# Retention and a squared-ReLU feed-forward on one core: outputs of the paired units in two steps, one weight block cast in four slices, and the decay of q moved to the evacuation of x

## The chip, the cores and the metric

The kernel runs on one core of a Trainium2 chip. A core has TensorE (PE; its weight loads are listed apart as PEld), VectorE (DVE), ScalarE (ACT), GpSimd (POOL) and SyncE (SP), which issues the transfers here. All of them run their own instruction streams in order and meet at semaphores. The metric is the device time of one execution in microseconds (us). Six executions of the kernel before took 293.09 to 294.34 us, with a median of 293.74.

## The reference, cut to what matters

```python
# q, k, v: (8, 8, 576, 64) float32;  w_in: (512, 2048);  w_out: (2048, 512)
scores = matmul(q, k^T) / sqrt(64)
gamma  = 1 - 2 ** (-5 - arange(8))                       # one decay per head
Dmat   = where(i >= j, gamma ** (i - j), 0)              # causal, decaying
attn   = matmul(scores * Dmat, v)                        # (8, 8, 576, 64)
x      = attn.transpose(0, 2, 1, 3).reshape(4608, 512)
h      = x @ w_in                                        # (4608, 2048)
out    = (max(h, 0) ** 2) @ w_out                        # (4608, 512)
```

## The kernel before, in words

**Units and groups.** The 4608 rows are cut into 36 units of 128 rows: four full chunks of a batch, and, for each two batches, a tail unit with the last 64 rows of both. Two units make a group, so there are 18 groups. Units 0 to 7 (groups 0 to 3, `PAIRED = 8`) are "paired": two chunks of one batch are loaded together with even and odd rows side by side, cast, transposed on TensorE and treated as one. From unit 8 on, GpSimd casts k and q, multiplies v by a decay, and k and q are transposed by a transfer.

**Retention.** The decay gamma^(i-j) is split into gamma^i on the side of q and gamma^(-j) on the side of v (`vdec`, applied as v is cast). Within a chunk the scores (`psc`) are masked by VectorE to `rT` (or `rx`) and multiplied by v; across chunks a state R, updated by VectorE from the sums of k and v (`psS`), is multiplied by q. Both parts are added up in PSUM as `psO`, in 64x64 quads. Then `psO` is evacuated to `xT` in fp16. For paired groups the factor gamma^i (`gam_f`) is applied there, by VectorE (line 543). For later groups q itself is multiplied by it (`qdec`, lines 363 to 369, two GpSimd instructions per unit), and the evacuation is a plain cast, one unit of the group by ScalarE and the other by VectorE (lines 707 to 713).

**Outputs of a paired group.** One TensorE task (`fo`, line 521) does the inter part that reads the state after the pair's first unit or before it for the crossed row halves (`inter(1)`), a drain, the intra part (32 quads), and the other inter part (`inter(0)`). It waits for all masks and for R.

**Feed-forward.** `ph` (line 831) multiplies `w_in` by `xT`, sixteen blocks of four matmuls per group, 128x256 each. ScalarE takes the ReLU to `rl`; ScalarE or VectorE squares it to `gT`. For groups 0 and 1 the second product `po` is a plain one (line 869), one unit's sixteen matmuls after the other's. From group 2 on it is a Strassen scheme (line 920) with seven products, for which VectorE forms four sums (`gS`, line 897) and, once, four sums of weights (`wT`, line 782).

**Loads and weights.** SyncE issues the loads in one written order, `FIRST`: k, q and v of units 0 and 2 with the weight blocks w0 to w7 among and behind them, then units 4 and 6. w0 to w3 are the blocks of `w_in`, w4 to w7 those of `w_out`, 1 MB each. They and the paired loads share a ring of four staging buffers (`wst`), so a load is issued when the casts of the load four places ahead have ended. Each weight block is cast in two halves, one by GpSimd and one by ScalarE (lines 318 to 325).

**Order of work.** The order on every engine comes from a planner, `Schedule`: tasks carry an engine, a key, a planned duration, dependencies and resources, and a simulated list scheduler takes, whenever an engine is free, the ready task of the lowest key. The order found is then written out, and the hardware runs each engine's list in order. Forty warm-up matmuls (line 248) have the highest key and are taken when TensorE has nothing else. A changed duration or key can thus change the order of all that follows.

Of the kernel before, what the change touches and what calls it, by code (L numbers as in the profile page):

```python
# [9 lines left out]
FP32 = mybir.dt.float32  # L10
# [93 lines left out]
def kernel(  # L104
# [13 lines left out]
    P = 128  # L118
# [56 lines left out]
    lnscale = const.tile([P, 1], FP32, name="lnscale")  # L175
    nc.vector.memset(lnscale, math.log(scale))

    vdec, qdec = {}, {}

    def make_vdec(kind, pos):  # L180
        t = const.tile([P, H], FP32, name=f"vdl_{kind}")
        nc.vector.tensor_scalar(out=t, in0=lnrow, scalar1=pos, scalar2=None, op0=ALU.mult)
        if kind in ("full", "tail"):
            e = qdec[kind] = const.tile([P, H], FP32, name=f"qdec_{kind}")
            nc.scalar.activation(out=e, in_=t, func=ACTF.Exp, scale=-1.0)
        d = const.tile([P, H], FP32, name=f"vdec_{kind}")
        nc.scalar.activation(out=d, in_=t, func=ACTF.Exp, bias=lnscale, scale=1.0)
        vdec[kind] = d
# [30 lines left out]
    gam_f = const.tile([P, NP, P], FP32, name="gam_full")  # L219
    for hp in range(NP):  # L220
        nc.scalar.activation(out=gam_f[:, hp, :], in_=iota_f, func=ACTF.Exp, scale=lncol[:, hp:hp + 1])
    dec128 = const.tile([P, NP], FP32, name="dec128")
    nc.scalar.activation(out=dec128, in_=lnrow_R, func=ACTF.Exp, scale=128.0)

# [66 lines left out]
    def add_load_pair(name, u):  # L291
# [3 lines left out]
        def fn():  # L295
            if name != "q":
# [3 lines left out]
        loaded[name, u] = loaded[name, u + 1] = dma_task(0, 1.81 if loaded else 2.9, fn, acq=("wst",) if name != "q" else (),  # L300
                                                         after=2.1 + LAG.get(name + str(u), 0.0))

    def add_weight(i):
        fb = i % 4

        def fn():
            if i < 4:
                t = stage.tile([P, NP, 512], FP32, name=f"wi{fb}", tag="wst")
                nc.sync.dma_start(out=t, in_=w_in[:, fb * 512:(fb + 1) * 512].rearrange("(m p) f -> p m f", p=P))
            else:  # L310
                t = stage.tile([P, 4, DM], FP32, name=f"wo{fb}", tag="wst")
                nc.sync.dma_start(out=t, in_=w_out[fb * 512:(fb + 1) * 512, :].rearrange("(n p) m -> p n m", p=P))
            tile_of["w", i] = t
        t = dma_task(0, 2.75, fn, acq=("wst",), after=2.1 + LAG.get(f"w{i}", 0.0))
        dst = w_in16[:, :, fb * 512:(fb + 1) * 512] if i < 4 else w_out16[:, fb * 4:(fb + 1) * 4, :]

        halves = []
        for j, eng in enumerate(("POOL", "ACT")):
            rows, sl = (slice(0, 4), slice(256 * j, 256 * j + 256)) if i == 0 else (slice(2 * j, 2 * j + 2), slice(0, 512))

            def fc(eng=eng, rows=rows, sl=sl):
                s = tile_of["w", i]
                (nc.gpsimd.tensor_copy if eng == "POOL" else nc.scalar.copy)(out=dst[:, rows, sl], in_=s[:, rows, sl])  # L323
            key = -50 + i if i or j == 0 else -17.5
            halves.append(add(eng, key, 1.05 if eng == "POOL" else 1.0, fc, deps=[t]))
        sched.free("wst", halves)
        wcast[i] = halves

# [18 lines left out]
    def half(x):  # L347
        return slice(64 * x, 64 * x + 64)

    def add_unit(u, base):  # L350

        kind, b, c = units[u]
        tail = [tail_dec] if kind == "tail" else []

        def sorted_cast(op, out_, in_):
            op(out=out_.rearrange("p (n b a d) -> p n b a d", n=2, b=2, a=2),  # L356
               in_=in_.rearrange("p (n a b) d -> p n b a d", n=2, a=2))

        def fk():
            t = tile_of["kq", u] = cast.tile([P, 2, H * D], FP16, name="kq16", tag="kq16")  # L360
            sorted_cast(nc.gpsimd.tensor_copy, t[:, 0], tile_of["k32", u])

        def fq():
            for n in range(2):
                nc.gpsimd.tensor_tensor(  # L365
                    out=tile_of["kq", u][:, 1].rearrange("p (n b a d) -> p n b a d", n=2, b=2, a=2)[:, n],
                    in0=tile_of["q32", u].rearrange("p (n a b) d -> p n b a d", n=2, a=2)[:, n],
                    in1=qdec[kind].rearrange("p (n a b o) -> p n b a o", n=2, a=2, o=1)[:, n].to_broadcast([P, 2, 2, D]),
                    op=ALU.mult)

        def fv():
            t = tile_of["v16", u] = cast.tile([P, H, D], FP16, name="v16", tag="v16")
            nc.gpsimd.tensor_tensor(  # L373
                out=t, in0=tile_of["v32", u],
                in1=vdec[kind].rearrange("p (h o) -> p h o", o=1).to_broadcast([P, H, D]), op=ALU.mult)
        ck = add("POOL", base, 0.65, fk, deps=[loaded["k", u]], acq=("kq",))
        cq = add("POOL", base + 1, 1.2, fq, deps=[loaded["q", u], ck] + tail)
        cv = add("POOL", base + 2, 1.1, fv, deps=[loaded["v", u]] + tail, acq=("v16",))
        for what, t in (("k", ck), ("v", cv)):
            for w in gate.get((what, u), []):  # L380
                sched.need(w, t)
        T["casts", u] = [ck, cq, cv]
        sched.free("ld", [ck, cq, cv])
        def fx2():
            t = tile_of["kqT", u] = work.tile([P, 2 * NP, P], FP16, name="kqT", tag="kqT", bufs=6)
            nc.sync.dma_start_transpose(out=t, in_=tile_of["kq", u].rearrange("p x n -> p (x n)"))
        T["kqT", u] = [add("SP", -1, 2.7, fx2, deps=[ck, cq], acq=("kqT",), after=3.0, lag=LAG_T)]
# [56 lines left out]
    def add_ret_pair(g):  # L444
# [40 lines left out]
        for s in range(2):  # L485
            src = None if s == 0 and not carry else u + s - 1

            def fr1(s=s, src=src):
                r = tile_of["tmp", u + s] = work.tile([P, NP * D], FP32, name="stmp", tag="stmp", bufs=1)
                nc.vector.tensor_tensor(out=r, in0=rT["sum"][s][:, 0:256], in1=tile_of["R", src], op=ALU.add)  # L490

            def fr2(s=s, src=src):
                r = tile_of["R", u + s] = st_pool.tile([P, NP * D], FP16, name="R", tag="R")
                x = rT["sum"][s][:, 0:256] if src is None else tile_of["tmp", u + s]
                nc.vector.tensor_tensor(
                    out=r.rearrange("p (n d) -> p n d", d=D), in0=x.rearrange("p (n d) -> p n d", d=D),
                    in1=dec128.rearrange("p (n o) -> p n o", o=1).to_broadcast([P, NP, D]), op=ALU.mult)
            if src is not None:
                chain.append(add("DVE", base + 5.5 + s, 0.42, fr1, deps=[t] + chain[-1:] + [T["R", src]]))
                T["Rread", src].append(chain[-1])  # L500
                sched.free("ff", chain[-1:])
            chain.append(add("DVE", base + 5.6 + s, 0.5, fr2, deps=[t] + chain[-1:], acq=("R",)))
            if src is None:
                sched.free("ff", chain[-1:])
            T["R", u + s], T["Rread", u + s] = chain[-1], []
# [12 lines left out]
                 start=(g, s, col) not in begun)  # L518
            begun.add((g, s, col))

        def fo():
            tile_of["psO", g] = ps_ret.tile([P, 2, 512], FP32, name="psO", tag="prO")
            inter(1)
            nc.tensor.drain()
            for m in range(NP):
                for e in range(2):
                    for s, b in ((0, 0), (1, 1), (0, 1), (1, 0)):
                        h = 2 * m + b
                        put2(s, h, tile_of["vx", u][half(s), e, 64 * h:64 * h + 64],
                             rT[e][half(s), m % 2, 2 * (m // 2) + b, :], s)  # L530
            inter(0)
        t = add("PE", base + 24, 1.3, fo, deps=masked + [T["R", u]] + ([T["R", u - 1]] if carry else []), acq=("prO",))
        for s in range(2):
            sched.free("kqT", [t])
            sched.free("kq", [t])
# [156 lines left out]
    def after_outs(g, t1, t2, key):  # L692
# [11 lines left out]
        for u in us:  # L704
            s, at = groups[g].index(u), us.index(u)

            def fx(s=s, at=at, u=u):
                if ("x", g) not in tile_of:
                    tile_of["x", g] = x_pool.tile([P, NP, n * P], FP16, name="xT", tag="xT")
                (nc.vector.tensor_copy if at else nc.scalar.copy)(  # L710
                    out=tile_of["x", g][:, :, s * P:(s + 1) * P].rearrange("p n (c i) -> p c n i", c=2),
                    in_=tile_of["psO", g][:, :, cols(at)].rearrange("p c (n i) -> p c n i", i=64))
            T["x", u] = add("DVE" if at else "ACT", key, 0.68 if at else 0.6, fx, deps=[t2], acq=() if at else ("x",))
        sched.free("prO", [T["x", u] for u in us])

    def add_casts(g):
        for u in units_of(g):
# [90 lines left out]

    def wcast_of(fi):
        w = wcast[fi // 4]  # L810
        return w[:1] if fi < 2 else w

    def add_ff(g):
        us = groups[g]
# [245 lines left out]
```

## Time and profile before

| | |
|---|---|
| median of 6 executions | 293.74 us (293.09 to 294.34) |
| the profiled execution | 293.16 us, its span 291.4 us |
| TensorE busy | 284.1 us (98%), 4328 matmuls |
| VectorE busy | 192.6 us (66%) |
| ScalarE busy | 195.4 us (67%) |
| GpSimd busy | 110.9 us (38%) |
| granted TensorE clock | 1.0 |

The span runs from the first to the last instruction of the execution; the time of the execution is a little longer. Ends of matmuls are modelled, so the spacing of their starts says more than their busy time. A line of the timeline holds the start, the duration, the engine, the line of the program, the operation, output and inputs, and how many instructions were merged; in brackets stands the idle time ahead and what ended it. A line of the groups has the count, the busy time, the mean duration in ns, and behind the second bar the idle time of that engine just before, with what released it. A line of the waits reads: engine and work that waited, what it waited for, then total us, times and the longest.

### The profile page before, as it was taken

What the parts mean: (1) busy time and instruction counts of PE and PEld (TensorE: products, weight loads), DVE (VectorE), ACT (ScalarE), POOL (GpSimd) and SP (SyncE); (2) the same over time, 40 slices, a digit from 0 to 9 for tenths busy, and PEclk for the clock granted to TensorE, in tenths of its full rate; (3) what the DMA queues carried; (4) which work ended last, traced back from release to release, by engine and by line L of the source; (5) the groups of instructions that cost most, each with busy time, mean ns of one, the idle gap of its engine ahead of it and who ended that gap; (6) DMA issues with size and microseconds to landing.
All of it is one profiled execution on the core that took longest, in us unless ns stands there. A gap on an engine that the chain in (4) does not pass through costs nothing.

```text
span 291.4 us, 10092 instructions
## 1 busy us (share of the span) xinstructions
PE 284.1 (98%) x4328; PEld 234.2 (80%) x4328; DVE 192.6 (66%) x416; ACT 195.4 (67%) x370; POOL 110.9 (38%) x151
## 2 busy tenths in 40 slices
PE   8998999999999999999999999999999999999995
PEld 3557765688888889888888888888888888888884
DVE  3785579749484938644977767857695956465632
ACT  5456866397758585868676677686767676857830
POOL 5343454735536434462709080808080700000000
PEclk9999999999999999999999999999999999999999
DMA  7999999999999999999998798879796730201004
GB/s 201 328 367 385 369 280 255 241 215 180 238 209 225 172 165 212 224 218 208 179 205 164 173 191 191 183 180 195 180 186 173 145 94 2 74 2 73 2 0 146
DMA packets 139421, 54.14 MB, mean 186 GB/s; under 512 B 118128, under 2 KB 130928, under 8 KB 139376
## 3 DMA queue, kind: packets, MB, share of 16 engines
q1 hardware_dynamic: 139072, 53.23, 84.1%
q8 instruction: 34, 0.56, 0.8%
q10 hardware_dynamic: 304, 0.26, 0.3%
q14 instruction: 11, 0.09, 0.2%
HBM read 36.70 MB, written 9.44 MB: 158 GB/s over the span
## 4 chain that ended last, share of the span: by engine, by line
PE 84%; DMA 6%; DVE 3%; ACT 2%; SPq 1%; issue 1%; POOL 1%; DVEq 0%; POOLq 0%
PE ph L831 38%; PE po L920 32%; PE po L869 5%; PE psO L344 4%; DMA wi<-in_moe_w_in_dram 3%; DMA pair<-in_q_dram 2%; PE psc L344 2%; DVE gS L897 2%; PE psS L344 2%; SPq L299 1%; ACT gT L849 1%; ACT rl L839 1%; DVE gT L851 1%; POOL w_in L323 1%; PE psT L424 1%
## 5 line engine op out<-in xcount | busy, mean ns | idle before, releaser
L831 PE MATMUL ph<-xT,w_in 128*128 128x256 f16 x1152 | 139.7, 273 | 0.8 <-POOL w_in L323 0.8
L831 PEld LDWEIGHTS <-w_in 128*128 128x128 f16 x1152 | 110.9, 98 | 15.7 <-POOL w_in L323 1.3
L839 ACT ACTIVATE rl<-ph 128x512 f16<-128x512 f32 x144 | 84.3, 590 | 34.3 <-PE ph L831 32.1
L849 ACT ACTIVATE gT<-rl 128x512 f16<-128x512 f16 x104 | 65.8, 632 | 2.9
L365 POOL TENSOR_TENSOR kq<-q,qdec_full 128x256 f16<-128x256 f32 x48 | 33.9, 727 | 57.8 <-DMA q<-in_q_dram 57.8
L920 PEld LDWEIGHTS <-gS 128*128 128x128 f16 x512 | 49.1, 98 | 6.9 <-DVE gS L897 1.0
L920 PE MATMUL po<-wT,gS 128*128 128x256 f16 x384 | 52.6, 273 | 0.2
L897 DVE TENSOR_TENSOR gS<-gT,gS 128x512 f16<-128x512 f16 x64 | 34.8, 547 | 13.1 <-ACT gT L849 12.5
L897 DVE TENSOR_TENSOR gS<-gT 128x512 f16<-128x512 f16 x64 | 35.0, 549 | 10.0 <-ACT gT L849 9.9
L920 PEld LDWEIGHTS <-gT 128*128 128x128 f16 x384 | 37.3, 98 | 4.4
L920 PE MATMUL po<-w_out,gT 128*128 128x256 f16 x256 | 34.5, 273 | 0.0
L851 DVE TENSOR_TENSOR gT<-rl 128x512 f16<-128x512 f16 x40 | 20.9, 523 | 15.8 <-ACT rl L839 15.3
L373 POOL TENSOR_TENSOR v<-v,vdec_full 128x512 f16<-128x512 f32 x24 | 26.9, 1121 | 4.8 <-DMA v<-in_v_dram 3.8
L356 POOL CAST kq<-k 128x512 f16<-128x512 f32 x28 | 19.5, 698 | 21.0 <-DMA k<-in_k_dram 20.6
L933 ACT COPY u<-po 128x256 f32<-128x256 f32 x32 | 11.8, 370 | 20.0 <-PE po L920 19.8
L943 DVE TENSOR_TENSOR o<-po,u 128x256 f32<-128x256 f32 x31 | 13.1, 421 | 16.7 <-PE po L920 10.7
L649 DVE TENSOR_TENSOR rT<-psc,mask 128x512 f16<-128x512 f32 x28 | 18.3, 682 | 4.2 <-PE psc L344 4.2
L710 DVE CAST xT<-psO 128x512 f16<-128x512 f32 x14 | 9.7, 692 | 14.3 <-ACT xT L710 10.9
L920 PE MATMUL po<-w_out,gS 128*128 128x256 f16 x128 | 17.0, 273 | 0.0
L920 PE MATMUL po<-wT,gT 128*128 128x256 f16 x128 | 16.8, 273 | 0.0
L869 PE MATMUL po<-w_out,gT 128*128 128x512 f16 x64 | 15.8, 380 | 0.0
L710 ACT CAST xT<-psO 128x512 f16<-128x512 f32 x14 | 8.2, 586 | 9.6 <-PE psO L344 8.4
(85 smaller groups left out, 258.9 us busy)
## 6 DMA issues: line engine op xcount, KB each, us to landing
out_dram<-o SPq DMA_DIRECT2D x31, 256.0 KB, 3.4
k<-in_k_dram SPq DMA_DIRECT2D x24, 256.0 KB, 5.0
q<-in_q_dram SPq DMA_DIRECT2D x24, 256.0 KB, 4.8
v<-in_v_dram SPq DMA_DIRECT2D x24, 256.0 KB, 5.2
wi<-in_moe_w_in_dram SPq DMA_DIRECT2D x4, 1024.0 KB, 10.3
wo<-in_moe_w_out_dram SPq DMA_DIRECT2D x4, 1024.0 KB, 9.5
pair<-in_k_dram SPq DMA_DIRECT2D x4, 512.0 KB, 7.1
pair<-in_q_dram SPq DMA_DIRECT2D x4, 512.0 KB, 7.1
```

Source lines behind the costliest of these rows:

```text
L344: nc.tensor.matmul(out_, lhsT=lhsT, rhs=rhs, start=start, stop=True, skip_group_check=True, tile_position=(64 * row, 64 * col))
L356: op(out=out_.rearrange("p (n b a d) -> p n b a d", n=2, b=2, a=2), in_=in_.rearrange("p (n a b) d -> p n b a d", n=2, a=2))
L365: nc.gpsimd.tensor_tensor(out=tile_of["kq", u][:, 1].rearrange("p (n b a d) -> p n b a d", n=2, b=2, a=2)[:, n], in0=tile_of["q32", u].rea ...
L373: nc.gpsimd.tensor_tensor(out=t, in0=tile_of["v32", u], in1=vdec[kind].rearrange("p (h o) -> p h o", o=1).to_broadcast([P, H, D]), op=ALU. ...
L649: nc.vector.tensor_tensor(out=r, in0=tile_of["psc", g][:, :, cols(s)].rearrange("p a (n i) -> p a n i", i=64), in1=mask.rearrange("p (o r ...
L831: nc.tensor.matmul(tile_of["ph", g, fb][:, j, :], lhsT=w_in16[:, m, fi * P:(fi + 1) * P], rhs=tile_of["x", g][:, m, :], start=(m == 0), st ...
L839: nc.scalar.activation(out=t, in_=tile_of["ph", g, fb], func=ACTF.Relu)
L849: nc.scalar.activation(out=t, in_=rl, func=ACTF.Square)
L851: nc.vector.tensor_tensor(out=t, in0=rl, in1=rl, op=ALU.mult)
L869: nc.tensor.matmul(tile_of["po", u], lhsT=tile_of["g", g][:, fi, s * P:(s + 1) * P], rhs=w_out16[:, fi, :], start=(fi == 0), stop=(fi == N ...
L897: nc.vector.tensor_tensor(out=Sx(k, h), in0=in0(h), in1=in1(h), op=op)
L920: nc.tensor.matmul(tile_of["pb", g, bank], lhsT=left(i), rhs=right[:, i, :], start=(start and i == 0), stop=(i == HF - 1), skip_group_chec ...
```

## The change

1. Paired groups: `fo` becomes `fo1` (the intra part, which needs the masks and v but no state) and `fo2` (`inter(0)`, drain, `inter(1)`, which needs R). For units 0 and 1 the update of R gets a key behind the masks.
2. The second block of `w_in` is cast in four slices of 128 columns, in turn by GpSimd and ScalarE, and the four `ph` blocks of it wait each for its own slice only.
3. From unit 8 on, q is cast as k is, without decay; `qdec` and the two exponentials for it are gone, and the cast of a tail's q no longer waits for the tail's decay row. The evacuation of `psO` multiplies by `gam`, on VectorE for both units of a group, one after the other; PSUM is freed by the second.

```diff
-        if kind in ("full", "tail"):
-            e = qdec[kind] = const.tile([P, H], FP32, name=f"qdec_{kind}")
-            nc.scalar.activation(out=e, in_=t, func=ACTF.Exp, scale=-1.0)
...
+    gam = {"full": gam_f.rearrange("p n (c i) -> p c n i", c=2),
+           "tail": gam_f[:, :, 0:64].rearrange("p n (c i) -> p c n i", c=1).to_broadcast([P, 2, NP, 64])}
...
+    NARROW = (1,)
...
-        for j, eng in enumerate(("POOL", "ACT")):
-            rows, sl = (slice(0, 4), slice(256 * j, 256 * j + 256)) if i == 0 else (slice(2 * j, 2 * j + 2), slice(0, 512))
+        narrow = i in NARROW
+        for j, eng in enumerate(("POOL", "ACT", "POOL", "ACT") if narrow else ("POOL", "ACT")):
+            rows, sl = ((slice(0, 4), slice(128 * j, 128 * j + 128)) if narrow else
+                        (slice(0, 4), slice(256 * j, 256 * j + 256)) if i == 0 else (slice(2 * j, 2 * j + 2), slice(0, 512)))
...
-            key = -50 + i if i or j == 0 else -17.5
-            halves.append(add(eng, key, 1.05 if eng == "POOL" else 1.0, fc, deps=[t]))
+            key = -50 + i + 0.1 * j if i or j == 0 else -17.5
+            halves.append(add(eng, key, (1.05 if eng == "POOL" else 1.0) / (1.85 if narrow else 1), fc, deps=[t]))
...
         def fq():
-            for n in range(2):
-                nc.gpsimd.tensor_tensor(
-                    out=tile_of["kq", u][:, 1].rearrange("p (n b a d) -> p n b a d", n=2, b=2, a=2)[:, n],
-                    in0=tile_of["q32", u].rearrange("p (n a b) d -> p n b a d", n=2, a=2)[:, n],
-                    in1=qdec[kind].rearrange("p (n a b o) -> p n b a o", n=2, a=2, o=1)[:, n].to_broadcast([P, 2, 2, D]),
-                    op=ALU.mult)
+            sorted_cast(nc.gpsimd.tensor_copy, tile_of["kq", u][:, 1], tile_of["q32", u])
...
-        cq = add("POOL", base + 1, 1.2, fq, deps=[loaded["q", u], ck] + tail)
+        cq = add("POOL", base + 1, 0.62, fq, deps=[loaded["q", u], ck])
...
-            chain.append(add("DVE", base + 5.6 + s, 0.5, fr2, deps=[t] + chain[-1:], acq=("R",)))
+            chain.append(add("DVE", base + (6.5 if u == 0 else 5.6) + s, 0.5, fr2, deps=[t] + chain[-1:], acq=("R",)))
...
-        def fo():
+        def fo1():
+
             tile_of["psO", g] = ps_ret.tile([P, 2, 512], FP32, name="psO", tag="prO")
-            inter(1)
-            nc.tensor.drain()
             for m in range(NP):
...
+        def fo2():
             inter(0)
-        t = add("PE", base + 24, 1.3, fo, deps=masked + [T["R", u]] + ([T["R", u - 1]] if carry else []), acq=("prO",))
+            nc.tensor.drain()
+            inter(1)
+        t = add("PE", base + 23.9, 0.6, fo1, deps=masked + T["kvx", u], acq=("prO",))
+        t = add("PE", base + 24, 0.75, fo2, deps=[t, T["R", u]] + ([T["R", u - 1]] if carry else []))
...
-                (nc.vector.tensor_copy if at else nc.scalar.copy)(
+                nc.vector.tensor_tensor(
                     out=tile_of["x", g][:, :, s * P:(s + 1) * P].rearrange("p n (c i) -> p c n i", c=2),
-                    in_=tile_of["psO", g][:, :, cols(at)].rearrange("p c (n i) -> p c n i", i=64))
-            T["x", u] = add("DVE" if at else "ACT", key, 0.68 if at else 0.6, fx, deps=[t2], acq=() if at else ("x",))
-        sched.free("prO", [T["x", u] for u in us])
+                    in0=tile_of["psO", g][:, :, cols(at)].rearrange("p c (n i) -> p c n i", i=64),
+                    in1=gam[units[u][0]], op=ALU.mult)
+            T["x", u] = add("DVE", key + at, 0.7, fx, deps=[t2] + ([T["x", us[at - 1]]] if at else []),
+                            acq=() if at else ("x",))
+        sched.free("prO", [T["x", us[-1]]])
...
-        return w[:1] if fi < 2 else w
+        return w[fi % 4:fi % 4 + 1] if fi // 4 in NARROW else w[:1] if fi < 2 else w
```

More of the change, by code (lines that the diff above doesn't have):

```diff
@@ L176 @@
     nc.vector.memset(lnscale, math.log(scale))
-    vdec, qdec = {}, {}
+    vdec = {}
     def make_vdec(kind, pos):
```

## The prediction

> **What bounds the kernel now.** I read the page's first two parts first, then the chain that ended last, then the timelines of the first 40 us, then the waits, and last the groups that the change edits. From the page:
>
> ```profile
> PE 284.1 (98%) x4328; PEld 234.2 (80%) x4328; DVE 192.6 (66%) x416; ACT 195.4 (67%) x370; POOL 110.9 (38%) x151
> PEclk9999999999999999999999999999999999999999
> PE 84%; DMA 6%; DVE 3%; ACT 2%; SPq 1%; issue 1%; POOL 1%; DVEq 0%; POOLq 0%
> ```
>
> TensorE carries 84% of the chain at full granted clock. In the steady part it has hardly a hole: sixteen 128x256 matmuls take 1.75 us in the chain (`po` x16 at 241.82 minus 240.08), 109 ns each, whichever group they belong to. So two questions remain: when does that unbroken stream begin, and does the change open holes in it? TensorE's timeline of the head, lines that carry the answer:
>
> ```profile
> 20.20 1.04 PE L248 MATMUL warm<-junk 128*128 128x512 f16 x4
> 21.25 0.31 PE L344 MATMUL psO<-kqT,R 64*64 64x128 f16 x8
> 22.34 1.92 PE L831 MATMUL ph<-xT,w_in 128*128 128x256 f16 x16
> 24.67 2.36 PE L831 MATMUL ph<-xT,w_in 128*128 128x256 f16 x20 [0.41 <-POOL w_in L323]
> 27.38 3.23 PE L831 MATMUL ph<-xT,w_in 128*128 128x256 f16 x28 [0.35 <-POOL w_in L323]
> ...
> 36.53 1.91 PE L831 MATMUL ph<-xT,w_in 128*128 128x256 f16 x16
> 38.48 3.18 PE L869 MATMUL po<-w_out,gT 128*128 128x512 f16 x14
> ```
>
> And GpSimd's casts of the second weight block of w_in (20.81) and of the last block of w_out (37.16), with SyncE's issues of the w_out loads:
>
> ```profile
> 20.81 1.28 POOL L323 CAST w_in<-wi 128x1024 f16<-128x1024 f32 x1 [1.05 <-DMA wi<-in_moe_w_in_dram]
> 37.16 1.27 POOL L323 CAST w_out<-wo 128x1024 f16<-128x1024 f32 x1 [1.74 <-DMA wo<-in_moe_w_out_dram]
> 19.79 7.93 SPq L312 DMA_DIRECT2D wo<-in_moe_w_out_dram  x4
> 30.05 0.37 SPq L299 DMA_DIRECT2D pair<-in_k_dram  x1
> ```
>
> The reader is to see the coincidence at 38.4 us. By then TensorE has done every `ph` of groups 0 and 1 (16+16+20+28 and three times 16 make all 128) and the twelve `po` of unit 0 that the first three w_out blocks allow. The next `po` needs the last block, whose cast ends at 37.16+1.27 = 38.43; TensorE goes on at 38.48. Nothing else is open to it: the second unit's `po` are chained behind the first's, and units 4 and 5 are loaded behind the weights (their k is issued at 30.05; ScalarE casts it from 40.02). In the windows of 20 to 32 us the queue moves 385 to 386 GB/s with a busy share above 1, so the weights come at the memory queue's pace, one 1 MB block about every 2.7 us (casts at 20.81, 23.57, 26.28 and so on to 37.16).
>
> **The change, part by part.**
>
> *Two-step outputs and the later R of unit 0.* No instruction is added on TensorE. In the head, VectorE runs mask, R, mask (10.37 to 13.17); without the 0.41 us R between, the masks end some 0.33 earlier, and the intra part (32 quads, 0.64 us) runs in the time of warm matmuls. Group 1's intra part can use the warm slot at 20.20; only 16 inter quads (0.31 each eight) remain behind the R at 21.20. First stage outputs of group 0 come up to 1 us, those of group 1 some 0.4 us earlier.
>
> *Second w_in block in four slices.* A 128x512 cast takes 0.61 to 0.70 us on GpSimd (`kq<-k`) and 0.62 on ScalarE (`qx<-pair`), so the first two slices end near 21.45, the last two near 22.05; before, the halves ended at 21.83 and 22.09. TensorE can start `ph` of this block at 21.5 in place of 22.34, 0.9 us ahead, and fill the holes of 0.41 and 0.35 with group 1. The staging buffer is freed within 0.1 us of before, so the load that waits for it, the second of w_out, is issued as before.
>
> The sum of the head: up to 0.9+0.41+0.35 = 1.7 us ahead at 27.4, and all of it is given back waiting for the cast that ended at 38.43. I take 0. The only lever on the end is that cast itself: other GpSimd casts of that shape took 1.04, and this one 1.27 beside VectorE's `wT`. Ends: -0.23 if it runs alone, +0.23 if VectorE's two are both beside it.
>
> *q scaled no more by GpSimd, x scaled by VectorE.* The groups concerned, and the waits that decide:
>
> ```profile
> L365 POOL TENSOR_TENSOR kq<-q,qdec_full 128x256 f16<-128x256 f32 x48 | 33.9, 727 | 57.8 <-DMA q<-in_q_dram 57.8
> L365 POOL TENSOR_TENSOR kq<-q,qdec_tail 128x256 f16<-128x256 f32 x8 | 5.0, 648 | 8.7 <-DMA q<-in_q_dram 8.6
> L356 POOL CAST kq<-k 128x512 f16<-128x512 f32 x28 | 19.5, 698 | 21.0 <-DMA k<-in_k_dram 20.6
> L710 DVE CAST xT<-psO 128x512 f16<-128x512 f32 x14 | 9.7, 692 | 14.3 <-ACT xT L710 10.9
> L710 ACT CAST xT<-psO 128x512 f16<-128x512 f32 x14 | 8.2, 586 | 9.6 <-PE psO L344 8.4
> L543 DVE TENSOR_TENSOR xT<-psO,gam_full 128x512 f16<-128x512 f32 x8 | 5.4, 733 | 2.7 <-PE psO L344 2.7
> L649 DVE TENSOR_TENSOR rT<-psc,mask 128x512 f16<-128x512 f32 x28 | 18.3, 682 | 4.2 <-PE psc L344 4.2
> PEld L920 <- DVE gS L897: 1.0, 3, 0.4
> ```
>
> GpSimd: 56 multiplies of 38.9 us become 28 casts like those of k, 19.5 us; 19.4 us less. It waits 66 us for q's DMA, so nobody gains directly. ScalarE loses 14 casts, 8.2 us, and two 0.2 us exponentials. VectorE's 14 casts become 28 multiplies of 0.68 to 0.73: 19.1 to 20.5 less 9.7, so +9.4 to +10.8 us. That looks like a heavier VectorE, but its row shows 10.9 us of waiting for ScalarE's half, in 11 of 14 groups: the two casts ran one after the other, since both write one tile. Group 12: ScalarE 191.40 to 191.99, VectorE 192.03 to 192.72, 1.31 us for the pair; two multiplies back to back took 1.35 to 1.37 (groups 0 to 3). So x is complete at the same time within 0.06 us, and in those groups VectorE works where it stood idle. In groups 7, 9 and 10 VectorE cast first and ScalarE second; there VectorE's next work starts 0.65 later.
>
> VectorE also gets something back. Its `gS` sums take 0.42 with GpSimd idle (after 240 us) and 0.59 in the mean of 60 to 240 us; the time that GpSimd no longer spends on q comes off just there. The waits of TensorE for `gS` are three, of 0.08, 0.28 and 0.28 us in matmul spacing. I take half of these 0.64 as gone: -0.3; ends -0.64 and, if the longer VectorE order hits the tight groups, +1.9 (three groups, 0.65 each).
>
> *The intra and inter parts may be parted on TensorE.* Groups 2 and 3 (near 49 and 56 us) lie in the full stream. Going from full matmuls to 64x64 quads costs 0.09 us (eight `po` from 186.79 should end their issue at 187.66, the quads start at 187.75) and about 0.11 back. Both parts are keyed side by side, and R, keyed between the masks there, is ready before the last mask, so I take 0; ends 0 and +0.4 (two groups, 0.2 each).
>
> The Trainium skill ("TensorEngine Tiling (Array Packing)", Key Properties) says that a change of tiling mode drains the array, a rule that speaks against any parting of these outputs. Taken as a price for both groups, whatever the order of work, it would make the sum +0.1 in place of -0.3; the row prices the same trip at 0.2 us, but charges it only where full matmuls really come between.
>
> Sum: 0 - 0.3 + 0 = -0.3 us on the profiled execution of 293.16 (span 291.4 and 1.8 around it), 292.9. That execution is 0.6 below the median of 293.74; against the median the same sum gives 293.4.
>
> **The rivals.** *First, faster:* the head's lead is kept. It would be if the last w_out block landed earlier, or if TensorE had other work at 37 us. For it: GpSimd and ScalarE do wait for the weights' DMA before each cast, so every earlier landing counts. Against: the queue is full, the buffers come free when they did. It decides if the last cast ends over 0.6 us before 38.43. Price: 0.9 to 1.7, mean 1.3, so 292.4; together with all `gS` waits gone, 291.9.
>
> *Second, slower:* VectorE becomes late for `gS`. Place: the second half of the S2 sum and the S1 sum in the joined groups 7, 9 and 10. At 199.78 TensorE resumed 0.05 us after VectorE's sum; there is no margin there. It decides where x starts on VectorE without the idle time in front and the margin of the following sum is under 0.65. Three groups make +1.9, 295.6; one or two, 294.4 to 295.0. Against: the planner is told 0.7 for each x, close to the 0.68 to 0.73 measured, and sums lie several us behind x in most groups (x at 191.4, sums to 200).
>
> *Third, nothing at all,* 293.7: no wait moves. It is in the forecast's own range.
>
> **How the numbers follow.** A measurement of this kernel tells about 0.2% from no change, 0.59 us. I give the forecast with the third rival 0.44, the first 0.24 and the second 0.32: a saving above 0.6 needs nearly every term at its best end, since the head's is capped; a loss has no such cap, as the whole order of work is laid out anew from changed durations. The forecast's own range is 293.4 less 0.5 and plus 0.8, so 292.9 to 294.2. The range for 8 in 10 reaches to the first rival's middle and nearly to the second's upper end: 292.2 to 295.4.
>
> **What would show it.** Right: the `ph` of the second block begins before 21.8; TensorE then stands still for 0.7 to 1.9 us in front of the `po` that needs the last w_out block, and resumes between 38.2 and 38.7; x pairs on VectorE of 1.3 to 1.4 us; `gS` nearer 0.5 than 0.59; the time from that `po` to the end 248 to 249 us. Wrong: `po` resuming before 37.9, waits of TensorE for `gS` or `xT` summing over 1 us, or quads in more places than before.

## The result and the profile after

The changed kernel takes 292.61 us (median of 23 executions, 292.28 to 293.19) against 294.25 for the kernel before (47 executions, 292.42 to 295.47): a ratio of 0.9952, 95% interval 0.994 to 0.9963, so 0.5% faster. The time lies in the forecast range of 292.2 to 295.4, but not in the case held likeliest, a change within 0.2%. Besides the median the spread changed: 3.1 us before, 0.9 us after.

The profiled execution of the changed kernel took 292.89 us, its span is 291.1. Its page:

```profile
PE 283.8 (98%) x4328; PEld 234.8 (81%) x4328; DVE 197.8 (68%) x430; ACT 187.0 (64%) x355; POOL 89.0 (31%) x124
PE 85%; DMA 9%; SPq 1%; POOL 1%; issue 1%; DVE 0%; DVEq 0%; POOLq 0%
L359 POOL CAST kq<-q 128x512 f16<-128x512 f32 x28 | 19.1, 684 | 50.1 <-DMA q<-in_q_dram 49.7
L712 DVE TENSOR_TENSOR xT<-psO,gam_full 128x512 f16<-128x512 f32 x28 | 18.9, 687 | 6.9 <-PE psO L347 6.8
```

GpSimd is busy 21.9 us less, ScalarE 8.4 less, VectorE 5.2 more. All 28 evacuations of x are VectorE multiplies of 687 ns, and none waits for ScalarE any more. TensorE's timeline of the head, after:

```profile
21.54 0.39 PE L247 MATMUL warm<-junk 128*128 128x512 f16 x1
21.86 1.06 PE L347 MATMUL psO<-kqT,R 64*64 64x128 f16 x16
22.85 7.16 PE L835 MATMUL ph<-xT,w_in 128*128 128x256 f16 x64
...
36.47 1.47 PE L835 MATMUL ph<-xT,w_in 128*128 128x256 f16 x12
38.51 3.18 PE L873 MATMUL po<-w_out,gT 128*128 128x512 f16 x14 [0.56 <-POOL w_out L326]
```

The two holes of 0.41 and 0.35 us are gone, and TensorE is through with its `ph` 0.5 us earlier. Then it waits for the cast of the last w_out block and goes on at 38.51; before it went on at 38.48. The head has given nothing to the end. Over all profiles this `po` starts at 38.29 to 38.51 with the new head (six of them) and at 38.30 to 38.53 with the old one (five).

The difference arises after that point. I took, from the trace, the start of each matmul and of the next, between full 128x128 ones, and counted as a **hole** what goes beyond 109 ns (216 for 512 columns) by more than 40 ns. After the `po` at 38.5 us the profiled execution of before has 0.64 us of holes, all in front of `po` that read `gS`; the changed kernel has none, and its waits hold no line of TensorE for `gS`. From that `po` to the start of the last matmul it is 249.12 us before and 248.36 after, a difference of 0.76.

That is only half of the 1.6 us between the medians. The rest is in what the profiled execution of before was: with 293.16 us it lay near the fast end of its 47 times. A second profile of the same kernel shows more, in the first experiment below.

### The profile page after: what moved, and what is told of

Its sections match the earlier page's. It is cut to its first block, busy times and chain, and to the rows that moved or that the text cites. A ratio compares the mean times of both kernels' runs of the same rounds, so it can differ in the third digit from the quotient of the medians.

```text
span 291.1 us, 10066 instructions
## 1 busy us (share of the span) xinstructions
PE 283.8 (98%) x4328; PEld 234.8 (81%) x4328; DVE 197.8 (68%) x430; ACT 187.0 (64%) x355; POOL 89.0 (31%) x124
## 4 chain that ended last, share of the span: by engine, by line
PE 85%; DMA 9%; SPq 1%; POOL 1%; issue 1%; DVE 0%; DVEq 0%; POOLq 0%
PE ph L835 39%; PE po L924 34%; PE po L873 4%; PE psO L347 4%; DMA wi<-in_moe_w_in_dram 4%; DMA wo<-in_moe_w_out_dram 3%; DMA pair<-in_q_dram 3%; PE psc L347 2%; PE psS L347 2%; SPq L298 1%; POOL w_out L326 1%; PE psT L422 1%; POOL w_in L326 0%; DVE o L947 0%; POOL qx L407 0%
## 5 line engine op out<-in xcount | busy, mean ns | idle before, releaser
L901 DVE TENSOR_TENSOR gS<-gT,gS 128x512 f16<-128x512 f16 x64 | 33.9, 535 | 12.0 <-ACT gT L853 11.3
L359 POOL CAST kq<-q 128x512 f16<-128x512 f32 x28 | 19.1, 684 | 50.1 <-DMA q<-in_q_dram 49.7
L371 POOL TENSOR_TENSOR v<-v,vdec_full 128x512 f16<-128x512 f32 x24 | 26.3, 1096 | 17.7 <-DMA v<-in_v_dram 16.9
L359 POOL CAST kq<-k 128x512 f16<-128x512 f32 x28 | 18.5, 662 | 40.3 <-DMA k<-in_k_dram 40.0
L855 DVE TENSOR_TENSOR gT<-rl 128x512 f16<-128x512 f16 x40 | 18.8, 471 | 15.4 <-ACT rl L843 14.6
L712 DVE TENSOR_TENSOR xT<-psO,gam_full 128x512 f16<-128x512 f32 x28 | 18.9, 687 | 6.9 <-PE psO L347 6.8
L947 DVE TENSOR_TENSOR o<-po,p 128x256 f32<-128x256 f32 x17 | 7.2, 422 | 13.7 <-ACT u L937 7.9
```

Source lines behind the costliest of these rows:

```text
L371: nc.gpsimd.tensor_tensor(out=t, in0=tile_of["v32", u], in1=vdec[kind].rearrange("p (h o) -> p h o", o=1).to_broadcast([P, H, D]), op=ALU. ...
L712: nc.vector.tensor_tensor(out=tile_of["x", g][:, :, s * P:(s + 1) * P].rearrange("p n (c i) -> p c n i", c=2), in0=tile_of["psO", g][:, :, ...
L855: nc.vector.tensor_tensor(out=t, in0=rl, in1=rl, op=ALU.mult)
L901: nc.vector.tensor_tensor(out=Sx(k, h), in0=in0(h), in1=in1(h), op=op)
L947: nc.vector.tensor_tensor(out=o_tile(u)[:, half * HM:(half + 1) * HM], in0=bank(x), in1=tile_of[name, g], op=ALU.add)
```

## The experiments

The changes to the code are shown shortened, with `...` for what is left out. The theories: *relief*, that GpSimd's multiplies of q slow VectorE's sums and TensorE then waits for them; *margin*, that the earlier head keeps late transfers from reaching the end; and, later, *order*, that what counts is where the evacuation of x stands on VectorE and ScalarE.

**The kernel before once more.**

> The kernel before once more, for a second profile of it. Margin theory: where this execution is slower than the first profiled one (293.2 us), the added time lies before the po that needs the last w_out block (38.48 us there). Relief theory: it lies in waits for gS between 60 and 240 us.

It took 294.65 us, 0.4 above the median of the 47, of which 11 took at least as long. The `po` that needs the last w_out block starts at 38.48, as in the first profile to the hundredth. The holes behind it are 2.01 us, five of them: 0.33, 0.25, 0.29, 0.72 and 0.42 us at 142, 185, 200, 215 and 230 us. So two executions of one program, 1.49 us apart, differ by 1.37 us in these holes. The waits of this execution:

```profile
PEld L920 <- DVE gS L897: 2.6, 5, 0.8
```

The largest hole, on TensorE, VectorE and GpSimd (three parts of the timeline of this execution):

```profile
214.52 0.60 PE L831 MATMUL ph<-xT,w_in 128*128 128x256 f16 x4
215.68 0.61 PE L920 MATMUL po<-wT,gS 128*128 128x256 f16 x4 [0.55 <-DVE gS L897]
...
211.33 0.86 DVE L897 TENSOR_TENSOR gS<-gT,gS 128x512 f16<-128x512 f16 x1 [0.23 <-ACT gT L849]
212.11 0.83 DVE L897 TENSOR_TENSOR gS<-gT 128x512 f16<-128x512 f16 x1
212.86 1.26 DVE L897 TENSOR_TENSOR gS<-gT,gS 128x512 f16<-128x512 f16 x1
214.04 0.83 DVE L851 TENSOR_TENSOR gT<-rl 128x512 f16<-128x512 f16 x1
214.91 0.72 DVE L897 TENSOR_TENSOR gS<-gT,gS 128x512 f16<-128x512 f16 x1
...
211.29 1.37 POOL L365 TENSOR_TENSOR kq<-q,qdec_full 128x256 f16<-128x256 f32 x2 [6.74 <-DMA q<-in_q_dram]
212.62 1.22 POOL L373 TENSOR_TENSOR v<-v,vdec_full 128x512 f16<-128x512 f32 x1
213.79 0.80 POOL L356 CAST kq<-k 128x512 f16<-128x512 f32 x1
214.56 1.53 POOL L365 TENSOR_TENSOR kq<-q,qdec_full 128x256 f16<-128x256 f32 x2
```

The sum that starts at 214.91 on VectorE ends at 215.63, and TensorE, ready at 214.96, starts its `po` at 215.68. The five VectorE instructions shown took 0.72 to 1.26 us; with no GpSimd instruction beside them such a sum or square takes 0.42 (85 of them behind 60 us in the first profile, none above 0.426). And GpSimd works without a pause from 211.29, because q, its two multiplies, v and k follow one another. The same stretch in the changed kernel:

```profile
210.28 0.42 DVE L901 TENSOR_TENSOR gS<-gT,gS 128x512 f16<-128x512 f16 x1 [0.36 <-ACT gT L853]
210.62 0.42 DVE L901 TENSOR_TENSOR gS<-gT 128x512 f16<-128x512 f16 x1
210.96 0.83 DVE L901 TENSOR_TENSOR gS<-gT,gS 128x512 f16<-128x512 f16 x1
211.91 0.42 DVE L855 TENSOR_TENSOR gT<-rl 128x512 f16<-128x512 f16 x1
212.37 1.17 DVE L901 TENSOR_TENSOR gS<-gT,gS 128x512 f16<-128x512 f16 x1
...
210.64 0.87 POOL L359 CAST kq<-q 128x512 f16<-128x512 f32 x1 [5.61 <-DMA q<-in_q_dram]
212.22 1.04 POOL L371 TENSOR_TENSOR v<-v,vdec_full 128x512 f16<-128x512 f32 x1 [0.70 <-DMA v<-in_v_dram]
```

The cast of q ends before v has landed, and the square `gT`, most of it in the gap of 0.70 us, takes 0.42 in place of 0.83. The needed sum, slow here too (1.17 us), ends at 213.54, 0.38 before TensorE wants it:

```profile
213.92 0.60 PE L924 MATMUL po<-wT,gS 128*128 128x256 f16 x4
```

**The head alone.** The edit is the changed kernel with q and x as before:

```diff
-            sorted_cast(nc.gpsimd.tensor_copy, tile_of["kq", u][:, 1], tile_of["q32", u])
+            for n in range(2): nc.gpsimd.tensor_tensor(... in1=qdec[kind] ..., op=ALU.mult)
...
-            nc.vector.tensor_tensor(... in1=gam[units[u][0]], op=ALU.mult)
+            (nc.vector.tensor_copy if at else nc.scalar.copy)(...)
```

> The paired outputs in two steps and the sliced second weight block, with q still scaled by GpSimd and x evacuated by ScalarE and VectorE. Relief theory (the gain is that GpSimd's q multiplies no longer slow VectorE's sums, so TensorE's waits for them go): same as before within 0.2%, ratio 0.998 to 1.002. Margin theory (the gain is the 0.7 us that TensorE now has in hand ahead of the last w_out block, so that a late transfer no longer reaches the end): ratio 0.995 to 0.997, and the spread of the times shrinks as in the changed kernel (0.9 us against 3 us).

Measured: ratio 1.0 (0.9982 to 1.0019), times of 293.37 to 295.6, holes of 1.59 us in its profile. The margin theory falls: neither the median nor the spread moves with the two-step outputs and the sliced block.

**q and x alone.** The kernel before with part 3 of the change only.

> The kernel before with only q cast plainly and x scaled on VectorE; head as before. Relief theory: ratio 0.995 to 0.997 and no wait of TensorE for gS over 0.1 us. Margin theory: 0.998 to 1.002, spread of the times as before.

Measured: ratio 0.9945 (0.9925 to 0.9966), 292.53 to 293.35, holes of 0.05 us. The whole gain is in this part; without the head's edits it is as large as with them, within the intervals.

**GpSimd's load put back into the changed kernel.**

```diff
-            sorted_cast(nc.gpsimd.tensor_copy, tile_of["kq", u][:, 1], tile_of["q32", u])
+            for n in range(2): nc.gpsimd.tensor_tensor(... in1=ones8 ..., op=ALU.mult)
```

> The changed kernel, but GpSimd multiplies q by a row of ones in the two instructions of before, planned with the cast's 0.62 us, so that the order of work is that of the changed kernel and GpSimd is busy about 19 us more. Relief theory: most of the gain is lost, ratio to before 0.998 to 1.001. Margin theory: nothing is lost, 0.995 to 0.996.

Measured: ratio 0.9972 (0.9952 to 0.9991), 292.74 to 295.43, holes of 1.42 us. The spread of before is back, and of the gain of about 0.5% a half is lost, where the relief theory asked for most of it. Of the 1.42 us, 0.88 stand in front of a `po` that reads `gS` (at 82.8 us); the other 0.54, at 72.9, are in front of one that waited for an output sum of VectorE, which came behind a `gS` of 1.26 us. So GpSimd's load is a cause, but perhaps not the only one. The next two try the two main pieces of part 3, each alone.

**GpSimd's relief alone, in the order of before.**

```diff
-            for n in range(2): nc.gpsimd.tensor_tensor(... in1=qdec[kind] ..., op=ALU.mult)
+            sorted_cast(nc.gpsimd.tensor_copy, tile_of["kq", u][:, 1], tile_of["q32", u])
```

> The kernel before with GpSimd's two multiplies of q replaced by one plain cast, still planned with 1.2 us, so that the order of work on every engine is that of before; x is evacuated as before. This leaves the decay of q out of units 8 to 35. Relief theory (GpSimd's load alone): ratio 0.9945 to 0.996, no wait of TensorE for gS over 0.1 us. Order theory (what counts is where the evacuation of x stands in VectorE's and ScalarE's order): 0.998 to 1.001. Half from each, as the ones of the third run would suggest: about 0.997.

Measured: ratio 0.9974 (0.9961 to 0.9986), 292.39 to 293.91, holes of 0.34 us, the last at 142 us (0.08). The relief theory's 0.9945 to 0.996 is missed, and one hole (0.14 at 68 us) is above its 0.1; the half is met. About half of the gain comes from the load alone, with the instructions of VectorE, ScalarE and GpSimd in their old order.

**x on VectorE alone.**

```diff
+    gam = ones_x.rearrange(...).to_broadcast([P, 2, NP, 64])
...
-                (nc.vector.tensor_copy if at else nc.scalar.copy)(out=..., in_=...)
+                nc.vector.tensor_tensor(out=..., in0=..., in1=gam, op=ALU.mult)
-            T["x", u] = add("DVE" if at else "ACT", key, 0.68 if at else 0.6, fx, deps=[t2], ...)
+            T["x", u] = add("DVE", key + at, 0.7, fx, deps=[t2] + ([T["x", us[at - 1]]] if at else []), ...)
```

> The kernel before with both evacuations of x on VectorE, multiplied by ones, planned as in the changed kernel; q is still scaled by GpSimd. Relief theory: nothing gained or a little lost, ratio 0.999 to 1.003, since VectorE has 10 us more and GpSimd nothing less. Order theory: 0.9945 to 0.997. Half from each: about 0.997.

Measured: ratio 0.998 (0.9959 to 1.0), holes of 1.55 us in a profiled execution of 293.71. The interval touches no change and reaches to 0.996: a slower kernel is all but excluded, the size of a gain is not settled. The product of the two, 0.9974 times 0.998, is 0.9954, close to the 0.9952 of the whole, but with these intervals that proves little. So the second half of the gain stays open. This run takes x off ScalarE and puts it on VectorE at once, and nothing parts the two. A third piece of part 3 was not tried alone: the planner is told 0.62 us for q in place of 1.2. With 1.2, as here, 8 of VectorE's 404 instructions (memsets aside) and 21 of ScalarE's 354 stand elsewhere than in the run of q and x alone. The places of the holes hint that the order counts: at 200 and 215 us both profiles of before, the head alone and this run have holes; the changed kernel has none there even with GpSimd's load put back, by ones or by a second cast. That is one profile each for the two, and with four casts a hole is back, at 219.6 us.

**The changed kernel again, and with a last block in slices.**

> The changed kernel once more, on the same chip as the other three. Every theory: ratio 0.994 to 0.9965.

Measured: 0.9953 (0.9936 to 0.9971), 292.53 to 292.68, again no hole.

```diff
-    NARROW = (1,)
+    NARROW = (1, 7)
...
+            rows, sl = (slice(j, j + 1), slice(0, 512)) if narrow and i >= 4 else ...
+    def wout_of(fi):
+        w = wcast[4 + fi // 4]
+        return w[fi % 4:fi % 4 + 1] if 4 + fi // 4 in NARROW else w
...
-                f2.append(add("PE", base2 + NF * s + fi, 0.216, f, deps=[sq[fi // nf]] + wcast[4 + fi // 4] + f2[-1:],
+                f2.append(add("PE", base2 + NF * s + fi, 0.216, f, deps=[sq[fi // nf]] + wout_of(fi) + f2[-1:],
```

> The changed kernel with the last block of w_out too cast in four slices, one row of 128 each, in turn by GpSimd and ScalarE, and each po waiting for its own slice. If the po that needs this block is what gives the head's lead back, it starts near 37.85 in place of 38.51 and the time falls by 0.4 to 0.65 us against the changed kernel, ratio to before 0.992 to 0.994. If the lead is lost elsewhere as well, the time is that of the changed kernel within 0.2 us.

Its timeline shows the `po` that was to come earlier:

```profile
36.59 1.47 PE L840 MATMUL ph<-xT,w_in 128*128 128x256 f16 x12
37.96 3.74 PE L878 MATMUL po<-w_out,gT 128*128 128x512 f16 x16
41.54 0.61 PE L423 MATMUL psT<-ident,kx 128*128 128x128 f16 x8
```

It starts at 37.96, 0.54 before that of the changed kernel, but the time is the changed kernel's: 292.67 against 292.59 on the same chip, ratio to before 0.9954 (0.9937 to 0.9971). The transposes of units 4 and 5 start at 41.54, where they were at 41.52 and 41.37 in the two profiles of the changed kernel. Against the second profile of the changed kernel the lead is 0.39 at the last block, 0.26 at `po` 36, counted from 0 (44.16 against 44.42), and 0.05 at `po` 48 (48.79 against 48.84). Behind the last weight block stand the loads of units 4 and 5, and the lead is lost in the stretch of their retention. Which of their steps takes it was not tried.

**GpSimd's busy time as a dose.** The changed kernel, with the cast of q issued two and four times:

```diff
-            sorted_cast(nc.gpsimd.tensor_copy, tile_of["kq", u][:, 1], tile_of["q32", u])
+            for _ in range(2):    # 4 in the second run
+                sorted_cast(nc.gpsimd.tensor_copy, tile_of["kq", u][:, 1], tile_of["q32", u])
```

> The changed kernel, with GpSimd casting q twice (same values to the same place), planned as one cast, so the order of work stays. GpSimd is busy some 19 us more, as with the multiplication by ones, but with instructions of one input. If GpSimd's busy time is what makes VectorE's sums late: 0.5 to 1.3 us above the changed kernel, ratio to before 0.997 to 0.999. If only the two-input multiply does it: as the changed kernel, 0.994 to 0.9965.

> The same with four casts, GpSimd busy some 57 us more than in the changed kernel. If GpSimd's busy time is the cause: slower than before, ratio 1.002 to 1.012, with waits of TensorE for gS of several us between 60 and 240 us. If only the two-input form counts: as the changed kernel. A third possibility, that GpSimd itself becomes late for the transposes of q: waits in front of psc in place of gS.

Measured: 0.9974 (0.9955 to 0.9993) for two casts, the same as with the multiplication by ones, and 1.0127 (1.0101 to 1.0154) for four: 298.21 us, just above the expected 1.012. So it is GpSimd's busy time, in either form within the intervals, and the cost is far from proportional to it: the first 19 us cost 0.2%, the next 38 us 1.5%. From the profile of four casts, the busy line of its page:

```profile
PE 285.0 (96%) x4328; PEld 233.1 (79%) x4328; DVE 218.1 (74%) x430; ACT 187.9 (63%) x355; POOL 145.8 (49%) x208
```

its waits:

```profile
PEld L925 <- DVE gS L902: 6.6, 12, 1.3
```

and a group of VectorE's sums between 60 and 240 us:

```profile
L902 DVE TENSOR_TENSOR gS<-gT,gS 128x512 f16<-128x512 f16 x48 | 35.9, 755 | 7.9 <-ACT gT L854 7.5
```

Beside it, the same group of the changed kernel in the same stretch:

```profile
L901 DVE TENSOR_TENSOR gS<-gT,gS 128x512 f16<-128x512 f16 x49 | 27.6, 570 | 9.9 <-ACT gT L853 9.5
```

The sum grows from 570 to 755 ns with the work on VectorE unchanged, and TensorE waits for sums twelve times. The waits hold no line of TensorE for GpSimd's casts of k and q or for their transposes, so the third possibility did not come. The same group of the kernel before:

```profile
L897 DVE TENSOR_TENSOR gS<-gT,gS 128x512 f16<-128x512 f16 x48 | 28.0, 589 | 10.9 <-ACT gT L849 10.5
```

So the change itself shortened these sums little: both kinds of `gS` together had a mean of 589 and 618 ns in the two profiles of before and of 576 and 517 in the two of the changed kernel. The waits went all the same. The stretch above suggests why: it counts where the slow sums stand, not how slow all of them are in the mean. No run moved the slow sums about at one mean, so this is argued, not shown.

**All profiles together.** Time of the profiled execution, its holes behind the last w_out block, and the difference:

| kernel | GpSimd busy, us | time, us | holes, us | time less holes |
|---|---|---|---|---|
| before | 110.9 | 293.16 | 0.64 | 292.5 |
| before once more | 110.2 | 294.65 | 2.01 | 292.6 |
| head alone | 108.8 | 294.52 | 1.59 | 292.9 |
| changed, multiplied by ones | 108.5 | 293.93 | 1.42 | 292.5 |
| x on VectorE alone | 109.5 | 293.71 | 1.55 | 292.2 |
| changed, q cast twice | 107.8 | 292.52 | 0.31 | 292.2 |
| relief alone | 89.4 | 293.22 | 0.34 | 292.9 |
| q and x alone | 88.9 | 292.69 | 0.05 | 292.6 |
| changed | 89.0 | 292.89 | 0.00 | 292.9 |
| changed again | 90.6 | 292.56 | 0.00 | 292.6 |
| last block in slices | 90.2 | 292.88 | 0.44 | 292.4 |
| changed, q cast four times | 145.8 | 298.17 | 5.23 | 292.9 |

Without the holes every kernel here takes 292.2 to 292.9 us, a width of 0.7 where the changed kernel's own times have 0.9. So the profiled times differ, beyond these 0.7 us, by TensorE's waits in the full stream, mostly for `gS`.

## Why the prediction was right or wrong

*The head gives nothing.* Right. The lead of up to 1.7 us was put at 0 at the end because of the cast at 38.43; TensorE resumed at 38.51 after 0.72 us of standing still (spacing of the matmuls), within the 0.7 to 1.9 foretold, and the head alone measured 1.0. In the second profile of the changed kernel it stood still for 0.44 and resumed at 38.35. The cast ran alone this time (1.05 us, as in the row of 1.04), but its block had landed 0.25 later, so the lever of 0.23 did not show.

*The second block's `ph` before 21.8.* Wrong: 22.85. The slices were there (both engines began at 20.7, two slices in 1.14 to 1.17 us), but the planner put the inter part of group 1, with its drain, in front. The lead came from the two closed holes alone (0.57 and 0.51 in the spacing of the starts), less a start that was 0.51 later; since it was given back anyway, the sum didn't suffer.

*x on VectorE costs no time.* Right in its effect, wrong in a detail. In 9 of 14 groups the update of R stands between the two multiplies, in one an output sum, and the pair takes 2.54 to 2.61 us in place of 1.31, against the 1.35 foretold. No matmul waited for `xT`.

*The `gS` waits, -0.3 with ends of -0.64 and +1.9.* This is the step that failed, by its size. The waits went, all of them, as that term's better end had it; but they had been 0.64 us only in the execution that was profiled, and 2.0 us in the second, of 294.65 us. I read a term that varies from execution to execution off a single one, a fast one, and carried its sum over to the median as it stood. The 0.6 us by which the profile lay under the median of six (1.1 under that of the 47), noted and left unexplained, was more of the same term, as far as the two profiles show. The reason given with it fits only in part: `gS` was to come nearer 0.5 than 0.59 us, and it took 0.58 in the first profile of the changed kernel and 0.52 in the second, and the relief of GpSimd alone gave about half of the gain.

*The range.* That it held 292.6 is luck in part. Against the median of 293.74 the `gS` term's best end, -0.64, reaches 293.1 and no further; the range went down to 292.2 for the sake of the first rival, whose kept lead did not happen.

*The rivals.* The first, faster by a kept lead, had the direction and the wrong cause; its weight of 0.24 was too small for the direction. The second, VectorE late in groups 7, 9 and 10, did not come: there were no holes in these groups. Parting the outputs in groups 2 and 3 didn't happen either; intra and inter follow one another directly, from 49.30 and from 56.18.

## What to carry to other kernels

An engine that is idle for nearly two thirds of the time and off the critical path can still cost time, if it works beside another whose results are wanted at once: take work off it in the stretches where that other engine has no margin, and look at where its pauses fall as much as at its sum. When one kernel's times spread by 1% and the profiled execution lies at the fast end, profile a second one before pricing a wait: what varies between the executions is the term to look for. A lead won ahead of a transfer that everything waits for is worth nothing until the transfer itself moves, and then the next one stands behind it.

## What the runs showed of the hardware

VectorE's fp16 sums and squares of two SBUF operands, 128x512, took 0.41 to 0.43 us with GpSimd idle (85 of them behind 60 us in the first profile). Of the 66 that ran beside a GpSimd instruction there, 23 took no longer, 31 took 0.7 to 0.88 and eight 1.26. In the twelve profiles none that ran beside casts alone took over 0.88; longer ones, up to 1.29, came only where one of GpSimd's multiplies was at work. Multiplies with one operand in PSUM did not change: between 60 and 240 us masks took 681 ns before and 683 under four casts. The Trainium skill ("GPSIMD Engine Reference", Specifications) says that GpSimd's SBUF interface is shared with VectorE, with contention for VectorE instructions in a two-port mode or with two SBUF inputs. The runs agree on both sides, the sums slowed and the PSUM multiplies untouched, and they add the price, about a doubling for half of the sums that overlap.

That plain casts on GpSimd cost the kernel as much as two-operand multiplies of the same total time (0.9974 and 0.9972, each within 0.002) was not expected. Nor was it that the spread of one program's times, 3 us against 0.9, could come from when a side engine's bursts fall. That the bursts move with the landing of q's transfers is likely from the rows, where GpSimd waits for q ahead of each burst, but no run fixed these landings, so it stays open.
